# A two-layer kernel of long convolutions and dense blocks on one core: the whole program is recorded in pieces and emitted in the order of a table

## The chip, the cores and the metric

The kernel runs on one core of a Trainium2 chip. The core has five engines that run side by side, each with its own queue of instructions: TensorE (PE, matrix products), VectorE (DVE), ScalarE (ACT), GpSimd (POOL) and SyncE (SP), which here issues every transfer. They wait for each other by semaphores. SBUF is the working memory, PSUM takes the results of TensorE, and 16 DMA engines move data to and from DRAM. The metric is the device time of one execution in microseconds (us); less is better. Three executions of the kernel before took 2600.58, 2601.38 and 2606.57 us, the median being 2601.38.

## What is computed

Two kinds of layers alternate, A, B, A, B, each added to its input after a layer norm without weights (mean and variance over the 1024 channels). There are 2048 tokens of 1024 channels. Cut from the reference:

```python
# A: q is the normalized x
k_shift = sum over t < 4 of k_pad[:, t:t+S, :] * shift_k[:, 3-t]
kv = k_shift * v
y = causal_long_conv(kv, ssm_k) + kv * ssm_D      # length 2048, per channel
A = q * y
# B: x is the normalized x
h = einsum("bsd,df->bsf", x, w1) + b1             # 1024 -> 3584
h = relu(h) ** 2
B = einsum("bsf,fd->bsd", h, w2) + b2             # 3584 -> 1024

x = A_q
x = x + A(layernorm(x)); x = x + B(layernorm(x))
x = x + A(layernorm(x)); x = x + B(layernorm(x))
```

The long convolution `y` depends on k, v and the kernels alone, not on x, so it is the same for both A layers and is computed once.

## The kernel before

The tokens are cut into four blocks of 512, the channels into eight groups of 128, the hidden width 3584 into 28 tiles of 128. `ORDER` gives the sequence of (layer, block) pairs: (0,0), (1,0), (0,1), (0,2), (0,3), (1,1), (1,3), (1,2). Every wide product is made of three matmuls (`mm3`, L391 to L394): each operand is split into a high part, rounded to a shorter format, and the low remainder, and high x high, high x low and low x high are summed in PSUM.

**The dense steps.** `add`, `add_joint` and `add_ahead` write a list `steps`; the main loop at the end runs over it. A step `m1` multiplies one weight tile of w1 with the block's normalized, transposed rows (`xh`, `xl`); a step `m2` multiplies hidden rows (`rh`, `rl`) with a tile of w2. A full step is 12 matmuls of 128x128 by 128x512. The last four blocks are done as two joint pairs (`JS`, steps `ja` and `jb`), which share sums of weights and rows so that seven products do the work of eight.

**The weight stream.** `w_advance` (called once a step) keeps the weights ahead of the step that uses them: `w_load` issues the transfer to a `wr` buffer (8 of them; up to `W_LOAD` = 9 weights ahead), `w_hi` (L1138) makes the high part on ScalarE into a `whl` or `jr` buffer, `w_lo` (L1146) the low part on VectorE or GpSimd. Some split weights are stored by `w_store` and read back whole later (`whl<-wd_m`).

**The long convolution.** It is done in stages that fill in between the dense steps. `fwd_kv`, `fwd_x` and `fwd_g` transform a block of kv and of the kernel (transposes L492, matmuls L460 and L520, results on the DRAM tensors `xd` and `gd`). `fwd_g` first issues the loads of its kernel rows (`fg<-ssmR`, L501, and `fk<-kd`, L504), waits some ticks, and then uses them in L520. `prod_stream` loads `cx` and `cg`, multiplies them on GpSimd (L618), sums on VectorE (L623), folds (L770 to L775), transforms back on TensorE (L689, for later blocks by `inverse`) and stores to `yd`.

**Norms and rows.** `prep_a`, `prep_b`, `prep_rows` and `chain` make the rows of the next block: statistics on VectorE, a square root on ScalarE (L799), scaling, transposes on TensorE (L884, L1770) and the split into `xh` and `xl` (L1778, L1779). `relu2` (L1623 to L1631) turns a finished `m1` result into `rh` and `rl`. `evict` (L1681) adds a finished `m2` result to its rows `acc`.

**What sets the order.** The kernel is written in a mode in which each engine gets its instructions in the order in which the program calls them. Several things make that order: objects of the class `Later` (`lag`, `plag`, `slag`, `soon`, `behind`) that call a function so many ticks later; rates (`PACE`, `FWD_RATE`, `T_RATE`) by which the convolution's generators are advanced between the steps; and, for the first block alone, the class `Plan`, which collects tasks with costs and tries 400 orders (`first_block`, from L1186 on). Buffers are handed out by pools in rings: the n-th request for a name gets slot n modulo the ring's size, and its first writer waits until the earlier holder's users are done.

A piece of the main loop, where one step is put together:

```python
        else:
            lag.tick()
            w_advance(s, w)
        behind.tick()
...
        wh, wl = wts[w][:, 0], wts[w][:, 1]
...
            for kk in range(4):
                t = slice(kk * P, (kk + 1) * P)
                mm3(o[:, t0:t1], wh[:, t], wl[:, t], xh[:, 4 * i + kk, t0:t1], xl[:, 4 * i + kk, t0:t1],
```

## Time and profile before

| | |
|---|---|
| median of three runs | 2601.38 us |
| span of the profiled execution, first to last instruction | 2600.5 us |
| mean granted clock of TensorE | 0.998 |
| matmuls, weight loads | 12184 each |
| instructions of VectorE, ScalarE, GpSimd | 3053, 2020, 1194 |
| moved by the DMA engines | 792.82 MB, 305 GB/s |

The profile is one execution recorded by the chip's profiler. A page of it gives busy times, the span in 40 slices, the chain of work that ended last, and groups of instructions. Views of the trace give busy time by stretch, waits by who waited for whom, and instructions in order of time. Matmuls overlap in their pipeline, so that a row of 0.39 us for a wide matmul does not mean that one starts only every 0.39 us. A line "L520" is a line of the kernel before; PEld is the loading of the stationary operand.

### The profile page before, as it was taken

The numbers are of one execution on the slowest core, as the hardware profiler recorded it, in microseconds if no ns is written. First come the engines' busy times: TensorE is split into PE (matmuls) and PEld (weight loads), VectorE is DVE, ScalarE is ACT, GpSimd is POOL, SyncE is SP. The second block draws the span as 40 slices with busy tenths as digits, with TensorE's granted clock in tenths as the row PEclk, the third lists the DMA queues.
The fourth block names the chain that finished last, engine by engine and source line by source line (L and its number), as shares of the span: only waits on it lengthen the run. The fifth ranks groups of instructions, "written<-read, shape, count | busy, mean of one in ns | idle before, by whom it ended". The sixth has DMA issues, their size and how long they took to land.

```text
span 2600.5 us, 36797 instructions
## 1 busy us (share of the span) xinstructions
PE 2561.4 (98%) x12184; PEld 2150.3 (83%) x12184; DVE 1932.0 (74%) x3053; ACT 1143.7 (44%) x2020; POOL 1012.0 (39%) x1194
## 2 busy tenths in 40 slices
PE   8999999999999999999999999999999999999999
PEld 7887887788888888888888888888888888888887
DVE  7877888768897887778879667886678667765553
ACT  4454344344435332344223465564434566553332
POOL 3546776377673878746888200000300000003000
PEclk9999999999999999999999999999999999999999
DMA  8799989889999999899999879999988466679682
GB/s 277 248 326 315 310 285 302 310 311 360 372 341 359 348 354 364 292 314 344 342 391 386 279 265 301 342 346 362 360 293 304 175 229 235 230 262 376 214 290 81
DMA packets 405329, 792.82 MB, mean 305 GB/s; under 512 B 47505, under 2 KB 150545, under 8 KB 405138
## 3 DMA queue, kind: packets, MB, share of 16 engines
q1 hardware_dynamic: 405138, 790.47, 86.1%
q8 instruction: 96, 1.57, 0.2%
q14 instruction: 95, 0.78, 0.1%
HBM read 583.22 MB, written 207.09 MB: 304 GB/s over the span
## 4 chain that ended last, share of the span: by engine, by line
PE 67%; DMA 14%; DVE 9%; POOL 5%; issue 2%; SPq 2%; ACT 1%; DVEq 0%; POOLq 0%; ACTq 0%
PE p L392 19%; PE p L393 18%; PE p L394 18%; POOL cp L618 4%; DMA cg<-gd 3%; DMA wr<-w 3%; PE pt L393 2%; PE pt L394 2%; PE pt L392 2%; PE p L1223 2%; DMA whl<-wd_m 2%; DVE sm L623 1%; DMA fx<-kT 1%; DVE whl L1146 1%; DMA wd_m<-whl 1%
## 5 line engine op out<-in xcount | busy, mean ns | idle before, releaser
L618 POOL TENSOR_TENSOR cp<-cx,cg 128x256 f32<-128x256 f32 (+1 forms) x864 | 674.9, 820 | 280.9 <-DVE sm L623 140.5
L2007 POOL TENSOR_TENSOR acc<-acc,px 128x512 f32<-128x512 f32 x16 | 24.3, 1534 | 884.2 <-DMA rh<-rd 503.5
L392 PE MATMUL p<-xh,whl 128*128 128x512 f32 (+1 forms) x932 | 356.0, 382 | 2.6 <-ACT rh L1626 2.1
L1146 DVE TENSOR_TENSOR whl<-wr,whl 128x512 fp32r<-128x512 f32 x385 | 298.2, 779 | 80.0 <-ACT whl L1138 75.7
L394 PE MATMUL p<-xh,whl 128*128 128x512 f32 (+1 forms) x932 | 352.5, 378 | 0.0
L393 PE MATMUL p<-xl,whl 128*128 128x512 f32 (+1 forms) x932 | 352.3, 378 | 0.0
L1138 ACT CAST whl<-wr 128x512 fp32r<-128x512 f32 x397 | 243.0, 618 | 168.1 <-PE p L394 80.8
L623 DVE TENSOR_REDUCE sm<-cp 128x128 f32<-128x384 f32 (+5 forms) x288 | 249.2, 874 | 33.2 <-POOL cp L618 32.7
L392 PE MATMUL p<-whl,rh 128*128 128x512 f32 x648 | 256.1, 395 | 2.7 <-ACT fg L542 1.7
L394 PE MATMUL p<-whl,rl 128*128 128x512 f32 x648 | 252.7, 390 | 0.0
L393 PE MATMUL p<-whl,rh 128*128 128x512 f32 x648 | 252.5, 390 | 0.0
L392 PEld LDWEIGHTS p<-xh,whl 128*128 128x128 f32 x932 | 175.6, 188 | 35.4 <-ACT rh L1626 2.5
L394 PEld LDWEIGHTS p<-xh,whl 128*128 128x128 f32 x932 | 175.3, 188 | 33.0
L393 PEld LDWEIGHTS p<-xl,whl 128*128 128x128 f32 x932 | 175.5, 188 | 31.0
L1623 ACT ACTIVATE wr<-p,b1t 128x512 f32<-128x512 f32 x110 | 75.8, 690 | 233.6 <-PE p L394 231.4
L1631 DVE TENSOR_TENSOR rl<-wr,rh 128x512 fp32r<-128x512 f32 x112 | 98.8, 882 | 87.8 <-ACT rh L1626 82.2
L392 PEld LDWEIGHTS p<-whl,rh 128*128 128x128 f32 x648 | 122.1, 188 | 28.3 <-ACT fg L542 2.1
L394 PEld LDWEIGHTS p<-whl,rl 128*128 128x128 f32 x648 | 121.8, 188 | 25.9
L393 PEld LDWEIGHTS p<-whl,rh 128*128 128x128 f32 x648 | 121.9, 188 | 23.8
L770 POOL TENSOR_TENSOR sm<-sm 128x256 f32<-128x256 f32 x96 | 82.0, 867 | 81.7 <-DVE sm L623 81.6
L392 PE MATMUL p<-jr,rh 128*128 128x512 f32 x248 | 98.5, 397 | 0.9 <-ACT jr L1138 0.9
L1681 DVE TENSOR_TENSOR acc<-p,acc 128x512 f32<-128x512 f32 x120 | 77.3, 683 | 28.9 <-PE p L394 28.9
(488 smaller groups left out, 6282.6 us busy)
## 6 DMA issues: line engine op xcount, KB each, us to landing
whl<-wd_m SPq DMA_DIRECT2D x231, 512.0 KB, 6.9
wr<-w SPq DMA_DIRECT2D x379, 256.0 KB, 5.7
rh<-rd SPq DMA_DIRECT2D x168, 256.0 KB, 5.3
jr<-wd_m SPq DMA_DIRECT2D x60, 512.0 KB, 6.7
rd<-acc SPq DMA_DIRECT2D x120, 256.0 KB, 3.5
wr<-td SPq DMA_DIRECT2D x112, 256.0 KB, 5.2
wd_m<-whl SPq DMA_DIRECT2D x49, 512.0 KB, 6.6
cx<-xd SPq DMA_DIRECT2D x48, 512.0 KB, 6.7
```

Source lines behind the costliest of these rows:

```text
L392: PE.matmul(o, lh, rh, start=start, stop=False, skip_group_check=skip)
L393: PE.matmul(o, lh, rl, start=False, stop=False, skip_group_check=skip)
L394: PE.matmul(o, ll, rh, start=False, stop=stop, skip_group_check=skip)
L618: G.tensor_mul(pr[:, :, a:e].rearrange("p c i -> p i c"), xt[:, a:e], gt[:, j - a:j - e if e <= j else None:-1])
L623: V.tensor_reduce(sm[:, ty, jj], st["pr"], axis=AX.X, op=OP.add)
L770: E.tensor_add(s[:, k], s[:, k], s[:, 0])
L1138: A.copy(t[:, 0], raws[n]["t"])
L1146: ENG[e[n % len(e)]].tensor_sub(t[:, 1], raws[n]["t"], t[:, 0].bitcast(F32))
L1223: PE.matmul(o, lh, r, start=start, stop=stop)
L1623: A.activation(r, st["o"], AF.Relu, bias=b1t[:, st["f"]:st["f"] + 1])
L1631: V.tensor_sub(st["lo"], st["r"]["t"], st["hi"].bitcast(F32))
L1681: V.tensor_add(accs[tt][:, d], o, accs[tt][:, d])
```

## The change

No operation, shape, loop or constant of the schedule changes. What changes is when the calls reach the engines' queues.

The five engine handles are replaced by stand-ins (`Hand`) that write every call on a `Tape`. A piece is one call of ScalarE, VectorE, GpSimd or SyncE; calls of TensorE that follow each other on the tape and write the same buffer are one piece, and a whole dense step (between `tape.cut(True)` and `tape.cut()`) is one piece. Buffers are promised (`Lazy`) and really taken from the pool when a call that uses them is played; `Shelf` keeps the ring order of each name, taking earlier slots first. At the end of the program `tape.play()` issues the pieces in the order that `ORDERED` gives. An entry "n+k" of that table says: emit n pieces that follow each other, then go k places beyond the end of them (or back, with a minus sign). Decoded it is an arrangement of the numbers 0 to 9848, in which pieces stand up to 59 places later and up to 125 places earlier than they were recorded.

The identity matrix is made outside the tape, ahead of everything. Pools that were opened inside a `with` are opened when first used, and the first block's pool is closed when the pool `ml` is opened. The rest of the diff is indentation, from the removed `with`.

```diff
+ORDERED = (
+    "4+1 1-2 1+1 1+1 1-2 1+1 1+2 2+1 1+1 1-2 1+1 4+1 3+1 2-18 1+2 1-5 1+11 1+6 2-5 1+5 2+1 4+1 3+1 1+2 1-14 1-4 1+16 "
...
+)
+class Lazy:
+    def __init__(self, get, root=None):
+        self.get, self.real, self.root = get, None, root or self
+
+    def now(self):
+        if self.real is None:
+            self.real = self.get()
+        return self.real
...
+class Shelf:
...
+    def get(self, name, k):
+        n = self.firsts.index(name)
+        while self.made <= n:
+            self.put(self.firsts[self.made], 0)
+            self.made += 1
+        for i in range(k + 1):
+            self.put(name, i)
+        return self.rings[name][k].real
+
+class Tape:
...
+    def add(self, e, f, a, kw):
+        key = None
+        if e == "PE":
+            key = "whole" if self.whole else a[0].root
+            if self.open is not None and self.open == key:
+                self.units[-1][1].append((f, a, kw))
+                return
+        self.units.append((e, [(f, a, kw)], 1) if key == "whole" else (e, [(f, a, kw)]))
+        self.open = key
+
+    def order(self):
+        got, at = [], 0
+        for t in ORDERED.split():
+            n, sign, jump = re.fullmatch(r"(\d+)([-+]?)(\d*)", t).groups()
+            got += range(at, at + int(n))
+            at += int(n) + int(sign + (jump or "0"))
+        assert sorted(got) == list(range(len(self.units)))
+        return [(i, self.units[i][0]) for i in got]
+
+    def play(self):
...
+        for i, e in self.order():
+            for f, a, kw in self.units[i][1]:
+                getattr(self.engines[e], f)(*map(real, a), **{k: real(x) for k, x in kw.items()})
...
-    V, A, G, PE, SY = nc.vector, nc.scalar, nc.gpsimd, nc.tensor, nc.sync
+    tape = Tape({"V": nc.vector, "A": nc.scalar, "G": nc.gpsimd, "PE": nc.tensor, "SY": nc.sync})
+    V, A, G, PE, SY = (tape.hand(e) for e in tape.engines)
...
+        tape.cut(True)
         if k == "m1":
...
+            tape.cut()
...
     lag.flush()
+    tape.play()
```

## Prediction

> **What bounds the kernel now.** First the page: busy shares, the slices, and the chain that ended last.

> ```profile
> span 2600.5 us, 36797 instructions
> PE 2561.4 (98%) x12184; PEld 2150.3 (83%) x12184; DVE 1932.0 (74%) x3053; ACT 1143.7 (44%) x2020; POOL 1012.0 (39%) x1194
> PE   8999999999999999999999999999999999999999
> DMA  8799989889999999899999879999988466679682
> PE 67%; DMA 14%; DVE 9%; POOL 5%; issue 2%; SPq 2%; ACT 1%; DVEq 0%; POOLq 0%; ACTq 0%
> ```

> TensorE is the bound: 2561.4 of 2600.5 us. The change adds and removes no instruction, so what an order can win is TensorE's idle time, 2600.5 - 2561.4 = 39.1 us (1.5%), and whatever it loses at a reduced clock. VectorE at 74% and the DMA engines at nine tenths in most slices up to the 29th are close enough behind to make TensorE wait if they are served in a worse order. The table of 65 us stretches says where the idle time lies (columns: stretch, length, busy time and count of PE, PEld, DVE, ACT, POOL, granted clock, DMA share, GB/s):

> ```profile
> 0.00:65.00 65.00, 57.30 (x331) 51.93 (x332) 51.92 (x78) 27.85 (x47) 25.04 (x24) 1.00 0.84 277
> 195.00:260.00 65.00, 58.68 (x268) 48.77 (x267) 47.31 (x74) 27.02 (x51) 44.32 (x56) 0.95 0.95 315
> 455.00:520.00 65.00, 59.28 (x329) 50.42 (x328) 51.08 (x108) 25.66 (x44) 21.00 (x23) 0.97 0.86 310
> 650.00:715.00 65.00, 65.00 (x314) 54.88 (x313) 52.72 (x78) 28.89 (x53) 39.86 (x50) 1.00 1.04 372
> 1885.00:1950.00 65.00, 65.00 (x288) 53.84 (x287) 48.02 (x102) 23.44 (x44) 0.00 (x0) 1.00 0.81 292
> 2535.00:2600.00 65.00, 60.79 (x269) 50.02 (x267) 21.87 (x34) 14.65 (x26) 0.00 (x0) 1.00 0.24 81
> ```

> So TensorE idles 7.7 us in the first stretch, 6.3 us in the fourth, 5.7 us in the eighth, 4.2 us at the end, and nothing in stretches like the two quoted between. Two stretches also show a clock below 1.00.

> Next the waits of TensorE alone: who waits, for whom, us in total, times, longest. I sort them by what the waiting matmuls belong to. **Group A**, transposes and convolution matmuls that stand between the steps of the dense layers and are pieces of their own in the change:

> ```profile
> PE pt L520 <- DMA fg<-ssmR: 6.0, 1, 6.0
> PE p L1770 <- DVE xl L1779: 3.5, 2, 2.1
> PE pt L689 <- POOL sm L774: 2.9, 1, 2.9
> PE p L884 <- ACT wr L827: 0.7, 1, 0.7
> PE pt L689 <- DVE fg L550: 0.7, 1, 0.7
> ```

> These are 6.0 + 3.5 + 2.9 + 0.7 + 0.7 = 13.8 us in six stalls. **Group B**, waits inside a dense step, where only the feeding piece can be moved forward:

> ```profile
> PE p L392 <- ACT rh L1626: 2.1, 1, 2.1
> PE p L392 <- ACT fg L542: 1.7, 1, 1.7
> PE p L392 <- DMA whl<-wd_m: 0.9, 3, 0.5
> PE p L392 <- ACT jr L1138: 0.9, 1, 0.9
> PE p L393 <- POOL jr L1146: 0.8, 1, 0.8
> ```

> 2.1 + 1.7 + 0.9 + 0.9 + 0.8 = 6.4 us in seven stalls. **Group C**, the planned first block, where data arrive just in time:

> ```profile
> PE p L492 <- DVE fx L1262: 3.1, 4, 1.4
> PE p L1223 <- POOL xh L1292: 1.7, 1, 1.7
> PE p L1528 <- DVE xl L1537: 1.1, 1, 1.1
> PE p L1223 <- ACT fg L1266: 1.1, 2, 0.7
> PE p L325 <- POOL ident masks.py:199: 1.4, 1, 1.4
> ```

> The first four are 7.0 us; the fifth is the wait for the identity matrix at the very start, which no order shortens. **Group D** is the reduced clock behind two of the stalls. The timeline of TensorE (start, us) and one row of the chain:

> ```profile
> 235.26 3.52 PE L520 MATMUL pt<-fg,yh 128*128 128x256 f32 x8 [5.96 <-DMA fg<-ssmR]
> 272.85 1.73 PE pt L520 x8
> 494.23 0.62 PE L392 MATMUL p<-jr,rh 128*128 128x512 f32 x1
> 497.63 0.48 PE L394 MATMUL p<-whl,rl 128*128 128x512 f32 x1
> 498.65 0.39 PE L392 MATMUL p<-whl,rh 128*128 128x512 f32 x1
> 499.79 0.39 PE L394 MATMUL p<-whl,rl 128*128 128x512 f32 x1
> 232.00:238.00 6.00, 2.74 (x7) 2.23 (x8) 5.32 (x5) 1.63 (x3) 5.84 (x7) 0.50 1.03 390
> 494.00:498.00 4.00, 4.00 (x14) 3.18 (x14) 1.89 (x3) 2.12 (x4) 1.35 (x1) 0.57 0.12 45
> ```

> The eight matmuls of L520 took 3.52 us instead of the 1.73 us of the same eight later: 1.8 us lost at clock 0.50. Between 494.23 and 497.63 eight wide matmuls were started, 0.425 us apart; between 498.65 and 499.79 five, 0.228 us apart. The loss is 8 x 0.197 = 1.6 us. Group D is 3.4 us.

> [...]

> **The change part by part.** *Recording.* The calls are kept in a list and issued at the end, while the program is built; on the chip this costs nothing by itself, since the instructions and the buffers (still handed out in ring order) are the same. Instruction rows would have to change for this to cost time.

> *The table.* Read as numbers, it is a list of all 9849 pieces. The fewest pieces that must be lifted out to turn the old order into the new is 1051: 715 go later (by 7 places at the median, at most 59) and 325 earlier (by 2 at the median, at most 125). 9849 pieces in 2600.5 us are 3.8 per us, so a typical delay of 7 places is 1.8 us of the program and the largest advance 33 us. A passed piece matters only where it stands on the same engine's queue (or where a wait between engines hangs on it): of pieces split over five queues, a move of one or two places mostly passes strangers. 768 of the 1051 go at most 8 places, so most of the table touches few same-queue neighbours.

> *Where.* Of the 1051, 186 fall in the first 1000 pieces, 512 between 1000 and 4250, 16 between 4250 and 5000, 333 between 5000 and 7500, and 4 after that. By 3.8 pieces per us, which is rough since pieces are not spread evenly, the first thousand is about 0 to 265 us, 4250 to 5000 about 1120 to 1320 us, and everything from 7500 about 1980 us on; both the thinly and thickly moved parts contain stretches where TensorE has no idle time. The parts from 1980 us on are left as they are, and their idle time, the 4.2 us at the end included, stays.

> *Group A* is what an order cures most easily: postponing a waiting piece by one dense step (12 matmuls x 0.228 = 2.7 us) covers every stall of it except the 6.0. For that one the queue of SyncE has the row

> ```profile
> 229.91 0.33 SPq L501 DMA_DIRECT2D fg<-ssmR  x1
> ```

> and the data come 5.35 us later. L520 stood ready at 229.3 (235.26 - 5.96), before its load was even issued, so the load must come about 6 us earlier or the matmuls about two steps later. Both are within the distances that the table uses: 6 us is 23 places. Bounds for A with D: nothing won, or all 17.2 us. I take three quarters, 12.9 us, nearer to the full end since a piece of its own can simply give way to the step behind it.

> *Groups B and C.* In B the feeder has to pass others on ACT, POOL or SP, each of which then comes later; in C the chains are serial and start with loads. Bounds: nothing, or all 6.4 + 7.0 = 13.4 us. I take one third, 4.5 us.

> *New waits.* Whatever is postponed holds up what stands behind it: an eviction on VectorE keeps a PSUM bank, a VectorE subtraction keeps a weight buffer, which keeps a load in SyncE's queue. Where TensorE has no idle time today, moves can only lose. Bounds: nothing, or a long stall each time (6.0 + 1.8 us). The nearest rows are those of group B, 6.4 / 7 = 0.9 us; I take three such new stalls, 2.7 us.

> *Sum.* -12.9 - 4.5 + 2.7 = -14.7 us. The profiled span is 2600.5 us; the median of the three runs is 2601.38, 0.9 us above it. The forecast is 2601.4 - 14.7, rounded to **2587 us** (0.6% faster).

> **The rivals.** A measurement of this kernel can tell about 0.3% from no change, 7.8 us; that is the bound below.

> *The order hardly reaches TensorE.* The stalls move on to the next piece rather than go: a postponed piece is missed by its own consumer, and the six and seven stalls are replaced by others of the same size. For it: 333 moved pieces lie past 5000, where waits quoted in B come to little, and most moves are short. Against it: behind each stall of group A stands a dense step, and the waits of the dense steps (group B) are fewer and shorter, so most of them were ready to go first. Time 2594 to 2609, middle 2601.

> *All of it is cured.* A, B, C and D go, with no new waits: 17.2 + 13.4 = 30.6 us, 2571 us; range 2562 to 2577 with the small stalls not quoted. Against it: C's serial chains.

> *Slower: loads late in a full DMA stage.* In the three stretches quoted from 195 to 715 us the DMA engines are busy at 0.86 to 1.04, and the slices show nine tenths most of the way to the 29th of 40, so a load brought forward takes its time from another. Group B has three waits of TensorE on whl<-wd_m: this stream has no slack there. A load seven places later comes 1.8 us later. Each such load that ends in a stall costs up to 1.8 us; past ten of them (17.4 / 1.8) the gains are gone, and with eighteen, about one in sixty of all moved pieces, the time is 2601.4 - 17.4 + 32.4 = 2616 us, range 2609 to 2625. Against it: loads are issued up to nine weights ahead, and today's three waits sum to only 0.9 us.

> [...]

> **How the numbers follow.** The forecast, 2577.1 to 2593.5, has 0.53; all cured, 0.15; no reach, 0.16; slower, 0.16. The likeliest one's own range is 2577 to 2593. For 8 times in 10 I take 2570 to 2608: about half of "all cured" lies below it (0.07) and most of "slower" above it (0.13). Faster by over 0.3% is 0.53 + 0.15 = 0.68, within 0.3% 0.16, slower 0.16.

> **What would show it.** In the profile after: the same 12184 matmuls; the waits of TensorE without L520 for ssmR, or with under 3 us; no stretch at clock 0.95 or 0.97; L1770 and L689 gone from the list or below 1 us; the stretch from 1980 us on unchanged in busy time, with 4.2 us idle at the end. New rows of L392 behind whl<-wd_m or wr<-w, each of a microsecond or more, would show the slower rival; an equal sum of waits at other lines would show the rival of no reach. The prediction is wrong if TensorE's idle time falls by much less than 10 us, or if its busy time, not its idle time, is what changes.

## The result and the profile after

The changed kernel takes 2572.69 us (median of 4 runs, 2570.39 to 2574.46), the kernel before beside it 2603.98 (4 runs, 2600.58 to 2608.47): a ratio of 0.9877, 95% interval 0.9862 to 0.9892. That is 31.3 us by the medians; the two profiled spans differ by 2600.5 - 2570.9 = 29.6 us. The forecast was 2587, with 2577 to 2593 as its own range. The time fell outside that, inside the whole range (2570 to 2608), in the case "all of it is cured" (2562 to 2577). The direction came as forecast; the 14.7 us that were forecast are less than half of what was won.

The page of the changed kernel, its busy line, TensorE's slices, its clock and the chain:

```profile
span 2570.9 us, 36794 instructions
PE 2554.1 (99%) x12184; PEld 2149.0 (84%) x12184; DVE 1936.2 (75%) x3053; ACT 1139.5 (44%) x2020; POOL 1021.9 (40%) x1194
PE   9999999999999999999999999999999999999999
PEclk9999999999999999999999999999999999999999
PE 90%; DMA 4%; DVE 3%; POOL 1%; issue 1%; SPq 1%; ACT 0%; DVEq 0%; POOLq 0%; ACTq 0%
```

The instructions of the engines are the same. TensorE's idle time went from 39.1 to 2570.9 - 2554.1 = 16.8 us, so 22.3 of the 29.6 us are idle time; the other 7.3 are busy time, of which the forecast named 3.4 (group D). In the chain, TensorE now stands for 90% instead of 67%: what ended last hangs on transfers and other engines far less often.

TensorE's waits in the changed kernel (every line reads L310, the line of the tape that issues it, so tiles tell the pieces apart):

```profile
PE p L310 <- DVE fx L310: 2.7, 3, 1.7
PE p L310 <- DMA whl<-wd_m: 2.3, 1, 2.3
PE p L310 <- ACT fg L310: 1.6, 2, 0.9
PE p L310 <- POOL ident masks.py:199: 1.4, 1, 1.4
PE p L310 <- ACT fx L310: 1.4, 2, 0.7
PE pt L310 <- DMA fg<-ssmR: 1.0, 2, 0.6
PE pt L310 <- ACT xh L310: 0.9, 1, 0.9
PE p L310 <- DVE xl L310: 0.7, 2, 0.5
PE pt L310 <- DVE xl L310: 0.3, 1, 0.3
```

The 6.0 us for fg<-ssmR are 1.0; the waits for sm are gone, those for xl are 0.7 and 0.3 instead of 3.5, 1.1 and 0.5; of group B only whl<-wd_m is left, and it grew from 0.9 to 2.3 (the rows with fg stand at 10 and 107 us, in the first block). Where the time went, by stretch (same columns as before; first the kernel before, then the changed one):

```profile
0.00:130.00 130.00, 119.69 (x769) 109.97 (x770) 107.94 (x182) 55.18 (x98) 59.32 (x56) 1.00 0.79 262
130.00:300.00 170.00, 163.68 (x804) 139.11 (x804) 128.85 (x194) 78.92 (x144) 98.22 (x109) 0.98 0.95 321
300.00:450.00 150.00, 144.31 (x682) 120.56 (x681) 130.16 (x195) 64.38 (x118) 113.05 (x138) 1.00 0.90 294
450.00:530.00 80.00, 74.28 (x441) 64.69 (x441) 58.78 (x118) 34.38 (x60) 30.93 (x32) 0.98 0.83 297
530.00:1400.00 870.00, 865.82 (x4164) 728.13 (x4163) 710.52 (x1036) 330.09 (x596) 617.62 (x769) 1.00 0.96 349
```

```profile
0.00:130.00 130.00, 123.45 (x809) 114.92 (x810) 108.90 (x183) 57.39 (x102) 65.42 (x60) 1.00 0.83 272
130.00:300.00 170.00, 168.97 (x817) 142.73 (x816) 138.36 (x205) 77.30 (x141) 107.00 (x122) 1.00 0.98 334
300.00:450.00 150.00, 150.00 (x718) 126.24 (x717) 136.91 (x204) 72.08 (x133) 114.09 (x136) 1.00 0.95 312
450.00:530.00 80.00, 78.71 (x516) 71.68 (x515) 58.22 (x116) 39.15 (x67) 41.10 (x42) 1.00 0.86 306
530.00:1400.00 870.00, 867.25 (x4120) 727.76 (x4119) 716.31 (x1050) 318.25 (x581) 623.94 (x778) 1.00 0.97 353
```

TensorE is busy 3.8, 5.3, 5.7 and 4.4 us more in the four stretches up to 530 us, and only 1.4 us more in the 870 us behind them. The gain lies in the first fifth of the program, although the table moves pieces up to three quarters of it.

A sharper reading, used below, compares the moment at which TensorE starts **the same piece** in two profiles. The L520 that stalled started at 235.26 us before; in the changed kernel it is this row of the timeline:

```profile
224.35 1.97 PE L310 MATMUL pt<-fg,yh 128*128 128x256 f32 x8 [0.42 <-DMA fg<-ssmR]
```

So the lead there is 10.9 us, and its eight matmuls take 1.97 instead of 3.52 us, which adds 1.6.

### The profile page after: what moved, and what is told of

It reads as the page before. It is cut to its first block, busy times and chain, and to the rows that moved or that the text cites. A ratio compares the mean times of both kernels' runs of the same rounds, so it can differ in the third digit from the quotient of the medians.

```text
span 2570.9 us, 36794 instructions
## 1 busy us (share of the span) xinstructions
PE 2554.1 (99%) x12184; PEld 2149.0 (84%) x12184; DVE 1936.2 (75%) x3053; ACT 1139.5 (44%) x2020; POOL 1021.9 (40%) x1194
## 4 chain that ended last, share of the span: by engine, by line
PE 90%; DMA 4%; DVE 3%; POOL 1%; issue 1%; SPq 1%; ACT 0%; DVEq 0%; POOLq 0%; ACTq 0%
PE p L310 80%; PE pt L310 11%; DMA cg<-gd 1%; DMA wd_m<-whl 1%; POOL cp L310 1%; SPq L310 1%; DVE xl L310 1%; DMA whl<-wd_m 0%; DVE whl L310 0%; DMA jr<-w 0%; DMA jr<-wd_m 0%; DMA fg<-ssmR 0%; DMA gd<-fg 0%; DMA wr<-w 0%; DVE fg L310 0%
## 5 line engine op out<-in xcount | busy, mean ns | idle before, releaser
L310 POOL TENSOR_TENSOR cp<-cx,cg 128x256 f32<-128x256 f32 (+1 forms) x864 | 683.6, 829 | 258.4 <-DVE sm L310 154.0
L310 PE MATMUL p<-xh,whl 128*128 128x512 f32 (+1 forms) x1864 | 566.2, 380 | 2.3 <-DMA whl<-wd_m 2.3
L310 POOL TENSOR_TENSOR acc<-acc,px 128x512 f32<-128x512 f32 x48 | 70.2, 1478 | 893.5 <-DMA rh<-rd 504.7
L310 PE MATMUL p<-whl,rh 128*128 128x512 f32 x1296 | 403.5, 392 | 0.3 <-DVE acc L310 0.3
L310 PEld LDWEIGHTS p<-xh,whl 128*128 128x128 f32 x1864 | 344.4, 188 | 67.0 <-issue 2.7
L310 DVE TENSOR_TENSOR whl<-wr,whl 128x512 fp32r<-128x512 f32 x387 | 299.7, 780 | 86.6 <-ACT whl L310 85.6
L310 PE MATMUL p<-xl,whl 128*128 128x512 f32 (+1 forms) x932 | 352.4, 378 | 0.1
L310 ACT CAST whl<-wr 128x512 fp32r<-128x512 f32 x405 | 246.1, 618 | 144.9 <-PE p L310 68.1
L310 PEld LDWEIGHTS p<-whl,rh 128*128 128x128 f32 x1296 | 240.2, 188 | 48.3 <-DVE acc L310 0.6
L310 DVE TENSOR_REDUCE sm<-cp 128x128 f32<-128x384 f32 (+5 forms) x288 | 249.2, 874 | 27.3 <-POOL cp L310 27.0
L310 PE MATMUL p<-whl,rl 128*128 128x512 f32 x648 | 252.7, 390 | 0.0
L310 PEld LDWEIGHTS p<-xl,whl 128*128 128x128 f32 x932 | 175.5, 188 | 31.5 <-DVE xl L310 0.3
L310 POOL TENSOR_TENSOR sm<-sm 128x256 f32<-128x256 f32 x192 | 167.8, 880 | 82.3 <-DVE sm L310 78.1
L310 ACT ACTIVATE wr<-p,b1t 128x512 f32<-128x512 f32 x130 | 89.7, 690 | 246.2 <-PE p L310 242.6
L310 DVE TENSOR_TENSOR rl<-wr,rh 128x512 fp32r<-128x512 f32 x112 | 104.2, 930 | 83.7 <-ACT rh L310 77.6
L310 PE MATMUL p<-jr,rh 128*128 128x512 f32 x496 | 154.6, 393 | 0.0
L310 PE MATMUL p<-xh,jr 128*128 128x512 f32 (+1 forms) x472 | 145.4, 379 | 0.0
L310 PEld LDWEIGHTS p<-whl,rl 128*128 128x128 f32 x648 | 121.6, 188 | 25.9
L310 DVE TENSOR_TENSOR acc<-p,acc 128x512 f32<-128x512 f32 x152 | 99.1, 684 | 52.7 <-PE p L310 52.6
L310 PE MATMUL p<-whl,xl 128*128 128x512 f32 x528 | 128.6, 389 | 0.0
L310 PE MATMUL p<-rh,whl 128*128 128x512 f32 x336 | 117.1, 389 | 0.0
L310 PE MATMUL p<-rl,whl 128*128 128x512 f32 x336 | 117.1, 389 | 0.0
```

The lines of the kernel that those rows point to most:

```text
L310: getattr(self.engines[e], f)(*map(real, a), **{k: real(x) for k, x in kw.items()})
```

## The experiments

All use the changed kernel's tape; the edit is the string `ORDERED`, nothing else. "In the table's order" for one engine means that this engine's pieces follow each other as in the change, the others as recorded, and that pieces of different engines are merged so that every piece stands behind those whose buffers it needs. Of the 1051 lifted pieces a good part pass only strangers: counted within each queue, the table lifts 59 pieces on TensorE, 225 on VectorE, 107 on ScalarE, 110 on GpSimd and 317 on SyncE.

**Is it the order?** Theory: the order alone. Rival: recording and late buffers.

```diff
-ORDERED = ( "4+1 1-2 1+1 1+1 1-2 ...
+ORDERED = ( "9849" )
```

> Recording and emitting through the tape, but with the table 0 to 9848 in order. Theory (the order alone carries the gain): the time of the kernel before, 2600 to 2608 us, with the same long wait of 6.0 us for fg<-ssmR. Rival (the recording itself, for instance buffers that are taken at their first use, carries part of it): 2 us or more below the kernel before.

Measured: 2602.97 us against 2604.68, ratio 0.9992 (0.9983 to 1.0002). The recording is worth nothing; all of the gain is order.

**Which part of the program?** The table up to a place where it closes on itself (the first 2285 pieces stay among themselves), and its complement.

```diff
+ORDERED = ( "4+1 1-2 ... 1-2 1+1 7579" )       # e2_head
+ORDERED = ( "2286+1 2-3 1+2 ... 1218+1 3-4 1+3 16" )   # e3_tail
```

> The table as far as piece 2285, which TensorE reaches at about 530 us; all later pieces in their recorded order. Comparing when TensorE reaches the same piece in the two profiles, the changed kernel is 25.3 us ahead by then, of 28.7 us at the end. Theory (the gain is the stalls of the first fifth): 25 us faster than before, 2575 to 2582 us. Rival (the late moves are needed to keep what the early ones win, because buffers and queues are handed on): 10 to 18 us faster.

> The recorded order as far as piece 2285 and the table from there on. Theory: 3 us faster than before (28.7 - 25.3), so hardly to be told from it, and the stalls of 235, 413, 493 and 520 us still there. Rival (late moves matter by themselves): 10 us faster or more.

Measured: the head 2578.09, ratio 0.9894 (0.988 to 0.9909); the tail 2599.27, ratio 0.998 (0.9971 to 0.9989). They are 26.6 and 5.4 us below the kernel before, together 32.0, where the whole gave 31.3. The theories said 25 and 3. So the gain of the first 530 us needs nothing from the later moves to be kept, and the 641 later ones of the 1051 moves are worth 5.4 us.

**Whose queue?** SyncE's alone, then the other four without it.

> Only SyncE's queue, that is the order in which transfers are issued, as in the table; the other four queues as recorded. Theory (earlier loads carry the larger part, since the piece that stalled 6.0 us, L520, was not postponed in TensorE's queue, but its load stands three places earlier in SyncE's): the stall on fg<-ssmR below 4 us, 8 to 16 us faster. Rival (SyncE's queue is held up by what VectorE, GpSimd and ScalarE deliver, so its own order is worth little alone): 0 to 4 us faster.

> The queues of TensorE, VectorE, ScalarE and GpSimd as in the table, SyncE's as recorded: the complement of the run with SyncE alone, which was 24.6 us faster by the medians, of 31.3 us for the whole change. Theory (the two parts cure different stalls and add up): about 7 us faster. Rival (most stalls can be cured from either side, by a load that comes earlier or by work that steps aside): 14 to 22 us faster.

Measured: SyncE alone 2580.06, ratio 0.9904 (0.9887 to 0.992), 24.6 us faster, where the theory had 8 to 16: the order of transfers is worth more than was thought. The other four 2605.02, ratio 1.0004 (0.9994 to 1.0013): nothing. This was neither 7 us nor 14: the two halves do not add up. In SyncE's run the wait for fg<-ssmR is 0.6 us:

```profile
PE pt L257 <- DMA fg<-ssmR: 0.6, 1, 0.6
```

The waits for sm are 0.7 us together there, without any move of TensorE; of group A's longer stalls only the one for xl (493 us before, 475 here) is left at its full 2.15 us. In the other run TensorE keeps waits of the old size:

```profile
PE pt L279 <- DMA fg<-ssmR: 5.7, 3, 3.3
PE pt L279 <- ACT xh L279: 5.3, 1, 5.3
```

Its lead over the kernel before is 6.3 us at the piece that this one started at 500 us, and 0.4 us at 550: the second row, a wait for the next block's rows that ended at 519 us (the kernel before waited 1.4 us about there), and a reduced clock about it (0.96 from 450 to 530 us, 0.98 in the kernel before) gave nearly all of it back. Why those rows came late was not taken apart; that the new order of the feeding engines counts on loads which, in the old order of transfers, have not come yet would fit.

**One load, and one stretch of SyncE's queue.** These test why an order of transfers is worth so much. In the kernel before, the timeline of SyncE's queue (start, us to issue) shows two transfers for cx and cg that were not issued until 215.93 us, behind one of 212.47; four transfers of weights and results stood behind them:

```profile
212.47 0.32 SPq L719 DMA_DIRECT2D cg<-gd  x1
215.93 0.32 SPq L719 DMA_DIRECT2D cx<-xd  x1
216.30 0.43 SPq L719 DMA_DIRECT2D cg<-gd  x1
216.83 1.75 SPq L1125 DMA_DIRECT2D wr<-w  x1
218.62 0.43 SPq L1154 DMA_DIRECT2D wd_m<-jr  x1
```

Between 212 and 217 us SyncE's queue waits 2.7 us for GpSimd, at these loads. Over the whole run they are the ones that wait longest in that queue, for GpSimd to free their buffers.

```profile
SPq L719 <- POOL cp L618: 159.6, 54, 7.0
SPq L1134 <- PE p L394: 104.7, 74, 5.9
```

```diff
+ORDERED = ( "938+5 1-6 5+1 8905" )             # e6_one_load
+ORDERED = ( "881+2 7+1 6-15 1-2 1+8 1+6 6+1 9-10 1+9 25+3 3-6 3+3 1+1 7-8 1+7 8896" )   # e7_sp_window
```

> The recorded order with one piece moved: the load fg<-ssmR whose lateness is the 6.0 us stall stands three places earlier in SyncE's queue, as in the table. Theory (the load must only pass the three transfers before it): it is issued at about 227.5 instead of 229.9 us, the stall is 3.5 us instead of 6.0, and part of the loss at half clock goes: 2 to 4 us faster. Rival (the queue as a whole is late there, so that three places are worth less than a microsecond): stall still above 5 us, no change.

> The recorded order with SyncE's queue alone, and only in a stretch of 25 transfers, issued at about 210 to 232 us, arranged as in the table (15 of them lifted): the weight loads ahead of two transfers for cx and cg that waited 3.5 us at the head of the queue, and the load of the one-load run three places earlier. Theory (a transfer that waits at the head of SyncE's queue holds up all behind it, and the order is worth what stands behind such a wait): the stall on fg<-ssmR 2 us or less and no half clock behind it, 6 to 8 us faster. Rival (the earlier waits of the queue, at 194 to 200 us, are what makes it late): the stall 3 us or more, at most 4 us faster.

Measured: one load 2600.43 against 2603.91, ratio 0.9987 (0.9978 to 0.9997); the stretch 2597.27, ratio 0.9977 (0.9966 to 0.9987), 3.5 and 6.6 us, both as their theories said. The L520 of the two, first one load, then the stretch:

```profile
232.19 2.63 PE L220 MATMUL pt<-fg,yh 128*128 128x256 f32 x8 [2.30 <-DMA fg<-ssmR]
```

```profile
227.98 1.97 PE L220 MATMUL pt<-fg,yh 128*128 128x256 f32 x8 [1.49 <-ACT wr L220]
```

Three places for one load took the stall from 5.96 to 2.30 us. With the weight loads ahead of the two waiting ones as well, the load no longer ends the wait at all, and TensorE starts the piece 7.3 us earlier than before (235.26 - 227.98). The issue times in the stretch run show the queue itself: two weight loads go out at 210.46, ahead of the pair, instead of at 216.83 and 219.15.

```profile
210.46 1.03 SPq L220 DMA_DIRECT2D wr<-w  x2
213.13 0.33 SPq L220 DMA_DIRECT2D cg<-gd  x1
213.51 0.43 SPq L220 DMA_DIRECT2D cx<-xd  x1
```

The profiles also show why the medians win less than the piece did: the next stall grew. In the stretch run TensorE waits 4.28 us for sm at 407 us, where the kernel before waited 2.86. One cured place hands part of its gain to the next uncured one.

**Any shuffle?**

> SyncE's queue in an order made at random: 241 transfers lifted by distances like the table's (at most 10 places; the table lifts 317), over the same part of the queue, other queues as recorded. Theory (it matters which transfers stand before a waiting one): 0 to 30 us slower than before. Rival (the recorded order is merely a bad one and any shuffle of it loses the long stalls): faster by 5 us or more.

Measured: 2622.23 against 2603.91, ratio 1.0066 (1.0051 to 1.0081), 18.3 us slower. Moves of the same kind at random places, in the one such order that was tried, cost about three quarters of what SyncE's right ones win. TensorE was busy 72.01 of 80 us in the stretch from 450 to 530 (74.28 before) and 862.29 of 870 in the long one behind it (865.82), so it loses in places that had little idle time too.

**Does TensorE's own order matter?** The table for all queues but TensorE's.

> The table for SyncE, VectorE, ScalarE and GpSimd, TensorE's queue as recorded. So far: SyncE's queue alone 24.6 us faster by the medians, the four others without it 1 us slower, the whole 31.3 us faster. Theory (the last 7 us come from the engines that feed TensorE, now that the transfers are early; TensorE's own order is worth little): 28 to 32 us faster. Rival (as the prediction had it, TensorE's pieces must give way to the next step for the stalls at 493 and 520 us to go): 22 to 26 us faster, with 2 us and more of waits for xl and xh left.

Measured: 2580.58 against 2602.13, ratio 0.9916 (0.99 to 0.9933), 21.6 us faster; the theory fell, and the time lies at the rival's lower end (22 to 26). Without TensorE's 59 moves the run is no better than SyncE alone, and waits are left that the whole change does not have:

```profile
PE p L304 <- DVE xl L304: 2.5, 4, 1.2
PE p L304 <- ACT wr L304: 2.1, 2, 1.4
PE pt L304 <- ACT wr L304: 1.7, 1, 1.7
```

Of the first row, 1.2 and 0.5 us are the rival's waits for xl, at 473 us; the rows for wr stand at 808 to 850 us, where the kernel before waited 0.7. The whole change is 31.3 us faster, so TensorE's order is worth about 10 us on top of the others, less than half of it up to 550 us by the leads below; and with VectorE, ScalarE and GpSimd, but without SyncE, it was worth nothing. Whether TensorE's and SyncE's orders would do without those of VectorE, ScalarE and GpSimd was not tried.

The leads at the same piece (us ahead of the kernel before; the first column is when that one starts the piece) put these runs side by side, one profile of each:

```
before   whole  SyncE  four others  stretch  no TensorE  identity
 119      5.0    3.8       2.3        2.4       4.0        0.2
 274     12.5   11.4       1.3        8.9      10.8        0.3
 431     18.1   16.8       0.6        4.7      16.5       -0.9
 550     25.3   20.7       0.4        6.4      21.7       -3.0
1206     25.4   20.4       0.9        6.8      18.4       -3.8
2010     28.7   22.4      -0.8        6.8      20.7       -4.1
```

Up to 431 us SyncE's order does nearly all; between 431 and 550 us, where the next block's rows are transposed between the dense steps (L1770), the whole wins 7.2 and SyncE 3.9.

**Which transfers?** The waiting loads of cx and cg against all others.

> SyncE's queue alone, and in it only the loads of cx and cg are put where the table has them among the other transfers (about 100 transfers lifted of 317). They are the transfers that wait longest at the head of the queue, 159.6 us in all for GpSimd. Theory (the worth lies in what these waiting loads hold up): 12 to 20 us faster, half or more of SyncE's 24.6. Rival (it lies in the other transfers among themselves, the stores and the weights): 0 to 8 us faster.

> The complement: the other transfers of SyncE's queue in the table's order among themselves, cx and cg left at their recorded places among them (about 250 lifted). Theory: 4 to 12 us faster, less than the run with cx and cg alone. Rival: 16 us or more faster.

Measured: cx and cg 2595.37 against 2602.13, ratio 0.9971 (0.996 to 0.9981); the others 2590.95, ratio 0.9953 (0.9938 to 0.9968). That is 6.8 and 11.2 us of 24.6, together 18.0: the rest comes only with both. My theory that half or more lies in what cx and cg hold up fell. The cx and cg run cured most of the 6.0 us stall (1.7 left), the other run none of it:

```profile
PE pt L235 <- DMA fg<-ssmR: 1.7, 1, 1.7
```

```profile
PE pt L256 <- DMA fg<-ssmR: 6.1, 1, 6.1
```

So head-of-queue waits explain that place, where it was shown, but they are not the main part of SyncE's worth: at 119 us the other transfers alone are 3.7 us ahead, cx and cg 0.5. What the other moves do in detail (which load, behind which) was not taken apart further.

**Further from here?** One more load moved in the changed kernel.

```diff
-... 3+1 1-14 1+6 2+7 ...
+... 3+1 1-14 1+20 1-15 2+7 ...
```

> The changed kernel with one more piece moved: the weight load whl<-wd_m that TensorE waits 2.3 us for at 1264 us goes three places forward in SyncE's queue, ahead of two loads of cx and cg and of one of fk or yd that stand before it; transfers land one after the other there, 1.27 us apart. Theory: that wait is gone or below 0.5 us, 1 to 2.5 us faster than the changed kernel, which the median can hardly show but the wait can. Rival (its buffer is not free before, so it only blocks the queue): the wait stays at 2 us or grows.

Measured: 2572.46, ratio 0.9882 (0.9867 to 0.9896), against 0.9877 for the changed kernel: no difference. (The load passed two transfers, cx and cg; the expectation miscounted.) At that step the wait is gone, but TensorE now comes sooner to the next one and waits 1.70 us there, instead of 2.33, for the next weight:

```profile
1265.06 0.50 PE L311 MATMUL p<-xh,whl 128*128 128x512 f32 x1 [1.70 <-DMA whl<-wd_m]
```

In that part the DMA engines are busy throughout (share 1.02 in this row of the changed kernel). That this is why the next weight came no sooner was not shown.

```profile
1235.00:1300.00 65.00, 62.66 (x288) 52.05 (x288) 50.69 (x72) 16.64 (x30) 53.98 (x74) 1.00 1.02 391
```

## Why the prediction was right, and what it mis-sized

**The bound** was right: TensorE's idle and half-clock time was nearly all that was won, 25.7 of 29.6 us between the spans. The last 600 us stayed as they were, but for 0.8 us less idle time at the end.

**Groups A and D** (12.9 of 17.2 us taken). Of A's stalls 0.4 us are left, at L520, and D is gone with them (the slow stretches at 232 and 494 us do not come back): 16.8 us, so the term was 3.9 us too small. Its reason was half right. That a waiting piece of TensorE simply gives way is not what cured most of it: SyncE's order alone cured the stalls for fg<-ssmR and for sm, and left the one at 493 us. (One step of 2.7 us would not quite have covered the 2.9 us for sm either.) For the longest stall it was the load that had to move, as that part said:

```profile
219.14 0.46 SPq L310 DMA_DIRECT2D fg<-ssmR  x1
```

It is issued 4.8 us before L520 stands ready (224.35 - 0.42), where it came 0.6 us after; not by its own move alone: three places gave 3.7 us of the stall, the queue ahead of it the rest. TensorE's order is worth about the last 10 us, and only once the transfers are early.

**Groups B and C** (4.5 of 13.4 us taken) were mis-sized by as much, from a smaller term. Of B, ACT rh (2.1), ACT fg (1.7), ACT jr (0.9) and POOL jr (0.8) are gone; of C's 7.0 us 4.1 are left (2.7 for fx, 0.7 for fg, 0.7 for xl). That is 5.5 + 2.9 = 8.4 us, nearly two thirds instead of one: the step "the feeder has to pass others, each of which then comes later" held the feeders back far less than was taken.

**New waits** (2.7 us) had the right size: 0.95 and 0.34 us for xh and xl at 496 us, 0.61 us for fg<-ssmR at 286 us, and 1.4 us more for whl<-wd_m, 3.3 us in all.

**What no term had.** Small waits that were not quoted fell by 3.0 us, and the idle time at the end, which was to stay, by 0.8 us; busy time adds 3.9 us. So 16.8 + 8.4 - 3.3 + 3.8 + 3.9 = 29.6 us, the difference of the spans.

**Busy time.** 7.3 us less busy, 3.4 of it group D. The other 3.9 has no explanation that a run shows. Rows of matmuls are modelled ends, and a wide matmul behind a wait shows 0.50 instead of 0.39 us, so part of the waits counts as busy; that this is all of it was not shown.

**The rivals.** "All of it is cured" had 0.15, and its time came, 2571 us, but its reason only in part: the groups A to D with the new waits gave 21.9 of its 30.6 us, and that the total is so near is luck, made up by the small waits, the end and the busy time. "The order hardly reaches TensorE" is what the four queues without SyncE do (ratio 1.0004). "Slower" is what the random order is, by 18.3 us; the price named for it, 2616 us, was of the right size, for an order that is not this one, and whether by that rival's late weights was not taken apart. The chances were set by how hard each group looked to cure; that 410 of the 1051 moves stand in the first 530 us, which held most of the idle time, spoke for more.

## What to carry to other kernels

When one engine issues all transfers, its queue is a schedule of its own: try its order first, before that of the engines that compute (here it gave 24.6 of 31.3 us by itself). Transfers that wait at its head, and what stands behind them, are one place to look, though here the loads that wait longest were worth only 6.8 of 24.6 us. A better order of the four other engines can be worth nothing when the transfers keep theirs (here a ratio of 1.0004), for the next stall gives it back (a lead of 6.3 us at 500 us was 0.4 us at 550); try the queues together. And read what an order can win from idle time by place: here the first 530 of 2600 us held 28 of the 39 us, and the moves behind them were worth 5 us.

## What the runs showed of the hardware

The half clock did not come behind the same stalls in two profiles. The kernel with the table 0 to 9848 issues what the kernel before does, and stalls at the same places, but its profile has further stretches at clock 0.50:

```profile
413.50:416.90 3.40, 3.29 (x12) 2.70 (x12) 2.96 (x5) 0.38 (x1) 3.40 (x5) 0.50 0.76 245
522.70:526.10 3.40, 3.40 (x19) 3.40 (x18) 1.75 (x3) 0.64 (x2) 3.40 (x5) 0.50 0.74 255
1294.10:1297.50 3.40, 2.92 (x7) 2.37 (x8) 3.00 (x4) 2.82 (x6) 3.40 (x5) 0.50 1.02 414
```

The stall before the second of them is this one, 2.28 us:

```profile
521.47 1.26 PE L220 MATMUL p<-ident,wr 128*128 128x128 f32 x8 [2.28 <-DVE xl L220]
```

In the profile of the kernel before the stall there was 1.39 us and no slow stretch followed. At clock 0.50 the 3.40 us of this stretch, in which TensorE was busy throughout, hold 1.7 us of its work at full clock, so that, by this estimate, the stall of 2.28 us cost 2.28 + 1.7 = 4.0 us, and the one of 1.39 us no more than itself.

```profile
409.10:412.50 3.40, 1.50 (x7) 0.92 (x5) 2.94 (x5) 0.64 (x2) 3.40 (x5) 1.00 1.01 382
412.50:415.90 3.40, 2.02 (x12) 1.70 (x13) 2.27 (x4) 0.98 (x2) 3.32 (x5) 1.00 0.87 281
491.00:494.40 3.40, 1.25 (x10) 1.00 (x10) 2.73 (x5) 2.11 (x5) 2.50 (x2) 1.00 0.97 378
```

```profile
410.10:413.50 3.40, 0.28 (x2) 0.28 (x3) 3.40 (x5) 1.24 (x2) 3.32 (x5) 0.99 0.96 377
519.30:522.70 3.40, 1.23 (x10) 1.05 (x11) 1.29 (x2) 2.13 (x4) 3.40 (x3) 1.00 0.72 284
```

At 413 us the wait for sm lies across two steps in the kernel before, each with 1.5 us of work and more, and the clock stays; in the identity run it leaves 0.28 us of work in one step, and the next is slow. The steps ahead of the slow stretches at 494 and 522.7 us have 1.25 and 1.23 us of work. In the profile of the kernel before, cut into 760 such steps from 3 to 2597 us, TensorE was busy for less than 1.3 us in three, those from 228.2, 231.6 and 491.0 us (1.10, 0.00 and 1.25 us), and each of them was followed by a step at clock 0.50; the others have 1.5 us and more, and each of them was followed by a clock of 1.00, also the least busy, from 409.1, 1286.3 and 30.2 us (1.50, 1.69 and 1.73 us). The longest single stall ahead of 494 us was one of 2.15 us.

The identity run was 2597.81 to 2606.27 us in ten runs, the changed kernel, with few such stalls left, 2570.39 to 2574.46 in four; that the half clock makes the wider spread was not shown.
